# A new written order for the linear-attention and long-convolution kernel, with some VectorE steps moved and the inverse transform's last matmuls split off

## The chip, the cores and the metric

The kernel runs on one core of a Trainium2 chip. The metric is the device time of one execution in microseconds (us), the median of three runs. Before the change it is 296.54 us (runs of 294.0, 296.54 and 297.77). The profile is of one more execution of the same program; its own device time is not listed, its span from the first to the last instruction is 291.2 us.

## The reference, cut to what matters

```python
q, k, v: (8, 8, 576, 64)   w_phi: (64, 128)
w_proj: (512, 1536)        filter_fft: (576, 512)      w_out: (512, 512)

def phi(x):
    proj = x @ w_phi
    proj = proj - max(abs(proj), axis=-1)
    return concatenate([exp(proj), exp(-proj)], axis=-1)
q_p, k_p = phi(q), phi(k)
kv  = einsum('bhsf,bhsd->bhfd', k_p, v);  z = sum(k_p, axis=2)
x   = einsum('bhsf,bhfd->bhsd', q_p, kv) / (einsum('bhsf,bhf->bhs', q_p, z) + 1e-6)
x   = heads side by side, (8, 576, 512)
x1, x2, x3 = split(x @ w_proj, 3)
x2_conv = irfft(rfft(x2, n=576) * rfft(filter_fft, n=576), n=576)     # along the sequence
out = (x1 * x2_conv * x3) @ w_out                                      # float32
```

There are eight batches b. The kernel keeps bf16 operands and float32 sums.

## The kernel before, in words

The 576 positions are split as 64 groups of nine (t, j), and a batch's eight heads lie as four pairs v of heads. The real Fourier transform is a matmul with cosines and sines made on the chip in the opening (the steps `ang`, `frac` and `sin`, lines 420 to 475), folded twice so that only sums and differences of a quarter of the length are multiplied.

The program is one straight list of steps, the string `PLAN`, that `run` (line 1043) goes through once. A word such as `X1e,ACT,2,0@0` calls the method `X1e` with the engine ACT, batch 2 and part 0, on PSUM bank 0. Every step issues its instructions on its engine's queue in this order; each engine runs its own queue in order, and waits on the others by semaphores put in for every tile. So the written order fixes the order on each of TensorE (PE), VectorE (DVE), ScalarE (ACT), GpSimd (POOL) and SyncE (SP), and which PSUM banks are reused after which step. PSUM has eight banks; most steps take two of them in a pair. Most SBUF tiles have rings of two to six buffers (`RING`, line 25), others one.

One batch goes through these steps, those of two or three batches interleaved:

- `load` (GpSimd's queue) brings q, k and v and casts them; `trh` (SyncE's queue, line 607) transposes half of q or k by DMA. In the first batch `pt` and `pte` do that by TensorE and a copy.
- `Pk` (line 636), `Qn` (643), `Pkt` and `Qnt` (651), eight or four matmuls with 64 rows, project k and q. `maxk`, `maxq`, `maxkt`, `maxqt` (VectorE, 716) take the maxima of the absolute values, `ex,k` (ScalarE, 698) both exponentials.
- `mhi`, `mlo`, `trm` and `trme` split q's maxima into two bf16 parts and transpose them; `Pq` and `Pqt` (670 to 687) project q the other way round and subtract the maxima; `ex,q` and `exqt` follow.
- `em` (752) makes k's factors, `vs` (GpSimd, 758) scales v with them, `KV` (773, 72 matmuls of 64 rows) sums over positions, `KVe` copies.
- `NE` and `NEt` (787, 796) make numerator and denominator; `rc` and `xn` (VectorE, 801 and 806), and `rct` and `xnt` for the leftover positions, divide.
- `trx` and `trxt` (SyncE, 825 and 830) transpose the result by DMA for the projections `X1` and `X3` (917) and `X1t` and `X3t` (926).
- `f1` and `f2` (854 and 860) form sums and differences, on GpSimd mostly, and `Ft` (four matmuls of 64 rows, 869) and `Fs` (876) transform; `Fe` and `Xl` copy; `X2` (895) projects in the frequency domain, `Y1` (VectorE, 905) multiplies with the filter, `m3` (909) adds halves.
- `I` (970) transforms back, six matmuls for each quarter m of the features: for each half e two with the main frequencies (T0 and T2) and one with the leftovers T4. T4 holds the leftovers of both halves in its two sets of 64 rows, and `inv[:, 4 + e]` is zero in the rows of the other half. `Ie`, `Ip` and `Im` (988, 991) take sum and difference of the halves.
- `X1e` copies X1, `tm` (958) multiplies with X3, `ym` (1005) with the convolution, `O` (1016) is the last projection, `Oe` copies, `st` stores.

`wz` steps are matmuls on zeros in the opening that keep TensorE occupied. The filter's own transform (`fl_load`, `fa`, `fb`, `rev`, `Ff`, `H`, `He`) runs in the opening too. `fa` (GpSimd, 495) writes its sums `fs` into the memory of `turn`, which holds the angles until the `sin` steps have read them. The index tables `fr` and `nr` have tiles of their own.

Of the kernel before, what the change touches and what calls it, by code (L numbers as in the profile page):

```python
# [36 lines left out]
fl_load,1,1 pt,k,0,1,1@7 exz ex,k,m,0,1@2 maxk,0,0@4 maxq,0,1@0 fl_load,3,1 fl_load,2,0 ex,k,p,0,0@4
pt,k,0,1,0@0 load,v,0 ex,k,m,0,0@4 pt,q,0,1,1@1 load,k,1 fl_load,3,0 maxk,0,1@2 pte,ACT,k,0,1,1@7
fl_load,1,0 pte,DVE,q,0,1,0@6 pte,ACT,k,0,1,0@0 Qn,0,0@4 pte,ACT,q,0,1,1@1 load,q,1 fa,POOL,0
maxq,0,0@4 Pkt,0@6 Qn,0,3@0 trh,k,1,0 maxkt,0@6 ex,k,p,0,1@2 wz,24@4 wz,17@2 trh,q,1,0 Qnt,0@4  # L40
maxq,0,3@0 fa,POOL,1 em,p,0,0 exkt,p,0@6 Pk,0,2@0 exkt,m,0@6 Qn,0,2@2 ex,k,p,0,2@0 maxqt,0@4
Pk,0,3@6 maxq,0,2@2 em,m,0,0 ex,k,m,0,3@6 w_load,proj,2 mhi,0 ex,k,p,0,3@6 rev@4 maxk,0,2@0
vs,POOL,p,0,0 mlo,POOL,0 vs,POOL,m,0,0 ex,k,m,0,2@0 trm,0@2 trme,DVE,0@2 Pq,0,0@2 ex,q,p,0,0@2
Pq,0,1@0 maxk,0,3@6 fb,0@4 em,m,0,1 em,p,0,1 vs,POOL,p,0,1 fb,1@4 wz,11@6 wz,9@7 KV,0,0@6
ex,q,p,0,1@0 ex,q,m,0,1@0 ex,q,m,0,0@2 Pq,0,3@4 Pq,0,2@0 ex,q,m,0,3@4 KVe,DVE,0,0@6 vs,POOL,m,0,1
NE,0,0@6 rc,0,0@6 NE,0,1@2 xn,0,0@6 trh,q,1,1 ex,q,p,0,3@4 Ff,2@6 Pk,1,1@4 rc,0,1@2 xn,0,1@2
f1,POOL,0,0,0 maxk,1,1@4 ex,q,p,0,2@0 Ffe,ACT,2@6 KV,0,1@2 Qn,1,0@6 ex,q,m,0,2@0 wz,5@0
KVe,ACT,0,1@2 ex,k,m,1,1@4 Pk,1,0@2 maxq,1,0@6 ex,k,p,1,1@4 maxk,1,0@2 NE,0,3@0 rc,0,3@0 Ff,3@6
Ffe,ACT,3@6 NE,0,2@4 xn,0,3@0 trh,k,1,1 w_load,proj,0 ex,k,m,1,0@2 Ff,1@6 rc,0,2@4 ptx,0,3@0
xn,0,2@4 ex,k,p,1,0@2 ptx,0,0@1 ptxe,DVE,0,0@1 ptx,0,2@4 f1,POOL,0,0,1 ptxe,DVE,0,3@0 Qnt,1@2  # L50
ptxe,ACT,0,2@4 Ffe,ACT,1@6 maxqt,1@2 Pqt,0@0 exqt,p,0@0 exqt,m,0@0 Qn,1,3@4 Ff,0@6 Ffe,ACT,0@6
Qn,1,2@2 maxq,1,3@4 Pk,1,2@0 Qn,1,1@4 load,v,1 maxq,1,2@2 ex,k,m,1,2@0 maxq,1,1@4 trx,0,1 X1,0,3@6
load,k,2 Pkt,1@2 ex,k,p,1,2@0 w_load,proj,1 maxk,1,2@0 exkt,m,1@2 X1,0,2@7 maxkt,1@2 X1,0,1@4
X1e,ACT,0,2@7 X1e,ACT,0,3@6 mhi,1 NEt,0@0 H,0@5 rct,0@0 xnt,0,1@0 X3,0,1@6 H,3@7 X1e,ACT,0,1@4
f1,POOL,0,1,1 f1,POOL,0,1,0 em,p,1,0 xnt,0,0@0 f2,POOL,0,1,0 tm,0,1@6 load,q,2 f2,POOL,0,1,1
exkt,p,1@2 Ft,0,1,0@2 He,DVE,3,0@7 Fs,0,2@2 Hl,ACT He,DVE,3,1@7 Fs,0,3@0 X1,0,0@4 Fe,ACT,0,2@2
Fe,ACT,0,3@0 Ft,0,0,6@2 He,DVE,0,0@5 X1e,ACT,0,0@4 He,DVE,0,1@5 Pk,1,3@0 f2,POOL,0,0,0 f2,POOL,0,0,1
Fs,0,1@6 Fe,DVE,0,1@6 Fs,0,0@2 H,1@4 ex,k,m,1,3@0 Fe,ACT,0,0@2 He,ACT,1,1@4 X3,0,2@5 He,ACT,1,0@4
mlo,POOL,1 trm,1@6 maxk,1,3@0 em,m,1,0 Xl,DVE,0 trme,DVE,1@6 em,p,1,1 X3,0,0@7 H,2@2 X2,0,2@3
em,m,1,1 ex,k,p,1,3@0 tm,0,0@7 H,4@4 trh,k,2,0 He,DVE,4,0@4 tm,0,2@5 vs,POOL,p,1,0 Pq,1,0@6  # L60
He,ACT,2,0@2 X3,0,3@0 tm,0,3@0 ex,q,m,1,0@6 vs,POOL,m,1,0 KV,1,0@4 vs,POOL,p,1,1 trxt,0
vs,POOL,m,1,1 trh,k,2,1 ex,q,p,1,0@6 Pk,2,0@0 KVe,ACT,1,0@4 Pk,2,1@6 ex,k,p,2,1@6 ex,k,m,2,1@6
trh,q,2,0 late X2,0,3@2 Y1,0,2@3 trh,q,2,1 maxk,2,0@0 X1t,0@3 Y1,0,3@2 maxk,2,1@6 load,v,2 Pq,1,2@4
X1te,ACT,0@3 X2,0,0@3 Y1,0,0@3 X3t,0@2 tmt,0@2 X2,0,1@6 load,q,3 X2,0,4@7 Y1,0,1@6 ex,q,p,1,2@4
Pq,1,1@2 ex,k,p,2,0@0 ex,k,m,2,0@0 Y1,0,4@7 w_load,out ex,q,m,1,2@4 Qn,2,1@0 maxq,2,1@0 ex,q,p,1,1@2
ex,q,m,1,1@2 KV,1,1@4 load,k,3 Qnt,2@6 Pkt,2@0 Pqt,1@2 maxqt,2@6 maxkt,2@0 m3,POOL,0,1 KVe,ACT,1,1@4
exqt,p,1@2 Qn,2,0@6 NE,1,1@4 exqt,m,1@2 maxq,2,0@6 m3,POOL,0,0 rc,1,1@4 xn,1,1@4 I,0,2@2 em,p,2,0
NE,1,0@6 Ie,0,2@2 Im,0,2@2 rc,1,0@6 Ip,0,2@2 exkt,m,2@0 exkt,p,2@0 xn,1,0@6 I,0,0@4 Qn,2,2@2
Ie,0,0@4 Ip,0,0@4 I,0,3@0 vs,POOL,p,2,0 Pq,1,3@6 trh,q,3,1 Ie,0,3@0 ex,q,p,1,3@6 Im,0,0@4
ex,q,m,1,3@6 ym,POOL,0,2 Qn,2,3@4 maxq,2,2@2 Im,0,3@0 I,0,1@2 Ip,0,3@0 maxq,2,3@4 ym,POOL,0,0  # L70
f1,POOL,1,0,0 Ie,0,1@2 Im,0,1@2 NE,1,3@0 rc,1,3@0 Pk,2,3@4 Ip,0,1@2 ym,POOL,0,3 xn,1,3@0 NEt,1@6
trx,1,0 mhi,2 mlo,POOL,2 ex,k,m,2,3@4 NE,1,2@2 em,m,2,0 trm,2@0 trx,1,1 trme,ACT,2@0 Pq,2,1@0
rct,1@6 trh,q,3,0 ex,k,p,2,3@4 ym,POOL,0,1 vs,POOL,m,2,0 xnt,1,0@6 rc,1,2@2 xnt,1,1@6 xn,1,2@2
O,0,1@6 O,0,3@7 trx,1,3 maxk,2,3@4 Pk,2,2@4 ex,q,m,2,1@0 ex,q,p,2,1@0 Oe,DVE,0,1@6 ex,k,p,2,2@4
Qn,3,3@2 Pq,2,2@0 ex,k,m,2,2@4 f1,POOL,1,0,1 maxq,3,3@2 O,0,2@6 Oe,ACT,0,2@6 Oe,ACT,0,3@7
f1,POOL,1,1,1 maxk,2,2@4 load,q,4 KV,2,0@2 KVe,DVE,2,0@2 O,0,0@6 Qn,3,2@4 trx,1,2 Oe,DVE,0,0@6
maxq,3,2@4 Pq,2,0@2 f1,POOL,1,1,0 ex,q,p,2,2@0 X1,1,2@7 ex,q,m,2,2@0 ex,q,m,2,0@2 f2,POOL,1,0,1
trh,k,3,1 X1,1,3@6 ex,q,p,2,0@2 X1e,ACT,1,2@7 st,SP,0,2,1 em,m,2,1 Ft,1,0,4@0 f2,DVE,1,0,0
# [12 lines left out]
tm,1,1@3 rct,2@4 xnt,2,1@4 I,1,2@0 Qnt,3@2 xnt,2,0@4 Pk,3,2@6 ym,POOL,1,1 maxqt,3@2 Ie,1,2@0
Im,1,2@0 Ip,1,2@0 ym,POOL,1,0 X1,2,0@0 ym,POOL,1,2 Pk,3,3@2 Qn,3,1@4 ex,k,m,3,2@6 X1e,ACT,2,0@0
ex,k,p,3,2@6 X1,2,2@1 maxq,3,1@4 X1,2,1@0 mhi,3 f1,POOL,2,1,1 load,v,4 O,1,2@4 maxk,3,3@2
X1e,ACT,2,1@0 Oe,ACT,1,2@4 em,m,3,0 X1e,DVE,2,2@1 trh,k,4,0 maxk,3,2@6 f2,POOL,2,0,0 ex,k,p,3,3@2
O,1,3@0 O,1,0@1 mlo,POOL,3 f2,POOL,2,1,1 f2,POOL,2,1,0 Ft,2,0,6@4 Fs,2,1@6 Oe,ACT,1,0@1 Oe,DVE,1,3@0
Fe,DVE,2,1@6 ex,k,m,3,3@2 X3,2,0@0 tm,2,0@0 trm,3@1 Fs,2,0@4 O,1,1@2 Oe,DVE,1,1@2 vs,POOL,p,3,0
st,SP,1,2,1 vs,POOL,m,3,0 Fe,ACT,2,0@4 trme,ACT,3@1 Qnt,4@4 trh,k,4,1 Ft,2,1,0@6 Fs,2,3@0
Fe,ACT,2,3@0 Fs,2,2@6 em,m,3,1 Pq,3,1@2 vs,POOL,m,3,1 ex,q,m,3,1@2 maxqt,4@4 load,q,5 Qn,4,0@4
Fe,DVE,2,2@6 Pq,3,0@0 ex,q,p,3,0@0 X2,2,3@6 em,p,3,1 ex,q,p,3,1@2 trxt,2 ex,q,m,3,0@0 maxq,4,0@4
Y1,2,3@6 X3,2,1@7 tm,2,1@7 X2,2,2@4 Y1,2,2@4 Xl,ACT,2 trh,k,5,1 KV,3,0@2 Qn,4,2@0 KVe,ACT,3,0@2  # L100
maxq,4,2@0 Pq,3,2@4 Pk,4,1@6 ex,q,m,3,2@4 maxk,4,1@6 X2,2,0@2 ex,q,p,3,2@4 NE,3,1@0 rc,3,1@0
X2,2,1@3 ex,k,p,4,1@6 vs,POOL,p,3,1 xn,3,1@0 ex,k,m,4,1@6 KV,3,1@4 KVe,ACT,3,1@4 Pq,3,3@0 Y1,2,1@3
# [994 lines left out]
```

## Time and profile before

| | us |
|---|---|
| median of three runs | 296.54 |
| lowest, highest run | 294.0, 297.77 |
| the profiled execution's own time | not listed |
| its span | 291.2 |
| busy in it: PE, DVE, ACT, POOL | 274.0, 252.3, 221.9, 228.5 |

A row of the profile's groups gives line, engine, operation, tiles as out<-in, shapes and count, then busy us and mean ns of one, then the engine's idle time before them and what ended it. In the chain that ended last a piece has its start, its length and what ran. In a row of stages each engine has its busy us and the number of its instructions. Matmuls are pipelined, so their durations overlap; the distance between starts is what a step costs TensorE.

### The profile page before, as it was taken

The numbers are of one execution on the slowest core, as the hardware profiler recorded it, in microseconds if no ns is written. First come the engines' busy times: TensorE is split into PE (matmuls) and PEld (weight loads), VectorE is DVE, ScalarE is ACT, GpSimd is POOL, SyncE is SP. The second block draws the span as 40 slices with busy tenths as digits, with TensorE's granted clock in tenths as the row PEclk, the third lists the DMA queues.
The fourth block names the chain that finished last, engine by engine and source line by source line (L and its number), as shares of the span: only waits on it lengthen the run. The fifth ranks groups of instructions, "written<-read, shape, count | busy, mean of one in ns | idle before, by whom it ended". The sixth has DMA issues, their size and how long they took to land.

```text
span 291.2 us, 10275 instructions
## 1 busy us (share of the span) xinstructions
PE 274.0 (94%) x4336; PEld 194.8 (67%) x4336; DVE 252.3 (87%) x438; ACT 221.9 (76%) x367; POOL 228.5 (78%) x187
## 2 busy tenths in 40 slices
PE   6688999998999999999999999999999899999992
...
PEclk9999999999999999999999999999999999999998
...
GB/s 140 230 207 175 144 204 165 139 175 181 143 192 177 163 204 159 153 119 165 122 111 156 197 169 114 163 135 191 99 14 93 84 36 2 34 108 54 69 130 184
DMA packets 72319, 40.07 MB, mean 138 GB/s; under 512 B 52496, under 2 KB 67216, under 8 KB 72272
## 3 DMA queue, kind: packets, MB, share of 16 engines
...
q10 hardware_dynamic: 320, 0.52, 0.7%
...
HBM read 33.75 MB, written 9.44 MB: 148 GB/s over the span
## 4 chain that ended last, share of the span: by engine, by line
PE 71%; DVE 3%; ACT 2%; issue 1%; DVEq 0%; ACTq 0%
PE ps L917 17%; PE ps L895 11%; PE ps L1016 10%; PE ps L970 8%; PE ps L773 5%; PE ps L787 4%; PE ps L876 3%; PE ps L926 2%; PE ps L670 2%; PE ps L636 2%; PE ps L643 2%; PE ps L676 2%; PE ps L869 2%; DVE mq L716 1%; PE ps L796 1%
## 5 line engine op out<-in xcount | busy, mean ns | idle before, releaser
L917 PE MATMUL ps<-xT,wproj 128*128 128x256 bf16 x512 | 64.0, 273 | 0.2 <-DMA wproj<-in_moe_w_proj_dram 0.2
L917 PEld LDWEIGHTS <-wproj 128*128 128x128 bf16 x512 | 48.1, 98 | 9.0 <-DMA wproj<-in_moe_w_proj_dram 0.4
L1005 POOL TENSOR_TENSOR yT<-cv,x1s 128x576 bf16<-128x576 f32 x31 | 39.4, 1279 | 15.6 <-ACT es L988 7.7
L716 DVE TENSOR_REDUCE mq<-ps 128x8 f32<-128x1024 f32 (+1 forms) x40 | 43.7, 1112 | 3.5 <-PE ps L643 1.5
L716 DVE TENSOR_REDUCE mk<-ps 128x8 f32<-128x1024 f32 (+1 forms) x40 | 44.1, 1112 | 2.9 <-PE ps L636 1.6
L758 POOL TENSOR_TENSOR vm<-vn,vm 128x1152 bf16<-128x1152 bf16 x16 | 34.3, 2152 | 7.4 <-ACT vm L752 7.4
L758 POOL TENSOR_TENSOR vp<-vn,vp 128x1152 bf16<-128x1152 bf16 x16 | 34.4, 2155 | 4.6 <-ACT vp L752 4.5
L698 ACT ACTIVATE Eqp<-ps 128x1024 bf16<-128x1024 f32 x32 | 32.9, 1038 | 6.1 <-PE ps L676 6.0
L854 POOL TENSOR_TENSOR SD<-xn 128x512 bf16<-128x512 bf16 x28 | 31.9, 1153 | 6.2 <-DVE xn L806 4.7
L1016 PE MATMUL ps<-wout,yT 128*128 128x512 bf16 x140 | 34.8, 379 | 0.1
L860 POOL TENSOR_TENSOR xf<-SD 128x512 bf16<-128x512 bf16 x26 | 29.7, 1155 | 6.4 <-DVE SD L854 5.9
L698 ACT ACTIVATE Ekp<-ps 128x1024 bf16<-128x1024 f32 x32 | 33.2, 1036 | 1.1 <-PE ps L636 0.7
L698 ACT ACTIVATE Eqm<-ps 128x1024 bf16<-128x1024 f32 x32 | 32.6, 1037 | 1.6 <-PE ps L676 0.8
L698 ACT ACTIVATE Ekm<-ps 128x1024 bf16<-128x1024 f32 x32 | 33.1, 1033 | 0.8 <-PE ps L636 0.7
L895 PE MATMUL ps<-wproj,XF 128*128 128x512 bf16 x128 | 31.6, 379 | 0.3 <-ACT x1s L298 0.3
L991 DVE TENSOR_TENSOR cv<-es,ps 128x288 f32<-128x288 f32 x64 | 26.3, 445 | 5.7 <-ACT es L988 4.4
L909 POOL TENSOR_TENSOR T<-T,T 128x1024 bf16<-128x1024 bf16 x14 | 29.6, 2127 | 1.7 <-DVE r L801 0.8
L970 PE MATMUL ps<-inv,T 128*128 128x288 bf16 x192 | 28.1, 286 | 0.7 <-DVE mq L716 0.4
L958 DVE TENSOR_TENSOR x1s<-ps,x1s 128x512 bf16<-128x512 f32 x32 | 21.8, 685 | 2.5 <-PE ps L917 1.1
L298 ACT COPY o<-ps 128x512 f32<-128x512 f32 x20 | 11.8, 600 | 14.4 <-PE ps L1016 12.0
L806 DVE TENSOR_TENSOR xn<-ps,r 128x512 bf16<-128x512 f32 x32 | 21.9, 689 | 0.9
L298 ACT CAST x1s<-ps 128x512 bf16<-128x512 f32 (+1 forms) x33 | 17.4, 540 | 6.7 <-PE ps L917 3.2
...
## 6 DMA issues: line engine op xcount, KB each, us to landing
...
```

Of the source, the lines that this page charges most:

```text
L298: self.nc.scalar.copy(dst, src)
L698: self.nc.scalar.activation(e, p, AF.Exp, bias=0.0, scale=1.0 if g == "p" else -1.0)
L716: self.nc.vector.tensor_reduce(out=out, in_=src, axis=AX.X, op=ALU.max, apply_absolute_value=True)
L758: self.eng(eng).tensor_tensor(out=t[:, :, :, 0:64], in0=self.at("vn", b)[:, 2 * X:2 * X + 2], in1=t[:, :, :, 64:65].to_broadcast([128, 2, ...
L854: self.eng(eng).tensor_tensor(out=o[:, :, 2 * i:2 * i + 2, :], in0=x[:, :, 0:2, :], in1=x[:, :, 2:4, :], op=ALU.subtract if i else ALU.add)
L860: self.eng(eng).tensor_tensor(out=o[:, :, 2 * i:2 * i + 2, :], in0=x[:, :, 0:4:2, :], in1=x[:, :, 1:4:2, :], op=ALU.subtract if i else ALU ...
L895: self.mm(self.pb(0), l, w[:, kt, 512:1024], start=(kt == 0), stop=(kt == 3))
L909: self.eng(eng).tensor_tensor(out=Y, in0=Y, in1=self.at(f"T{2 * e + 1}", b), op=ALU.add)
L917: self.mm(o[:, d], w[:, kt, f0 + 128 * m:f0 + 128 * m + 128], y[:, 1, ::-1, ::-1] if d else y[:, 0], start=(kt == 0), stop=(kt == 3))
L970: self.mm(self.pb(e, 0, 288), l, inv[:, 2 * e + i if i < 2 else 4 + e, :], start=(i == 0), stop=(i == 2))
L1005: self.eng(eng).tensor_tensor(out=self.at("yT", b)[:, m, 0:SEQ], in0=self.turn_of("cv", (b, m)).rearrange("p x h t -> p (x h t)"), in1=sel ...
L1016: self.mm(self.pb(0), y[:, kt, 128 * c:128 * c + 128], w[:, kt, :], start=(kt == 0), stop=(kt == 3))
```

## The change

The written order is new from the first word to the last; the steps are the same but for these:

- Each of the 32 `I` steps becomes `Is` (the four main matmuls) and, at another place of the order, before or behind it, `It` (16 times) or `Iz` (16 times). `It` takes the leftovers as two matmuls of 64 rows, in different halves of the array; `Iz` as two of 128 rows, as `I` did. `opens` remembers which of the parts came first, and only that one clears the bank. `Ft` and `Fs` may come in either order in the same way.
- Steps on another engine, counted before and after: `Fe` on DVE 7 to 13, on ACT 25 to 19; `X1e` on DVE 7 to 4; `Oe` on DVE 15 to 13; `KVe` on DVE 4 to 3; `pte` on DVE 4 to 6; `trme` on DVE 3 to 5; `Ffe` on DVE 0 to 1; `He` on DVE 5 to 4; `Xl` on DVE 1 to 0; `X1te` on DVE 0 to 1; `yt` on DVE 1 to 2; `f2` on DVE 6 to 2, on POOL 26 to 30; `m3` on DVE 2 to 3, on POOL 14 to 13; `ym` on DVE 1 to 4, on POOL 31 to 28. `f1` stays at 4 on DVE, at other places.
- `fsx` is a tile of its own. `fs` lies in it, and so do `fr` and `nr`.
- In the order, `exz` (the exponential on a dummy) now comes ahead of `sin,9` (the sine on a dummy); k is loaded ahead of q; `trx` stands behind its `xn`, most within a few steps, and loads and transposes stand further ahead of their uses; the stores are spread otherwise.

```diff
 PLAN = """
-gz,DVE sin,9 fz,DVE cz,DVE,0 loadh,q,0,0 gi_nr cz,DVE,1 gi_part gi_col cols_a cols_b cols_h
-loadh,k,0,0 gi_fr ang,DVE,2 wz,23@0 wz,30@1 wz,31@0 wz,32@1 wz,33@0 ang,ACT,3 fl_loadt ident frac,3
...
-Pq,2,3@0 ex,q,p,2,3@0 rc,2,0@4 xn,2,0@4 vs,POOL,m,2,1 Qn,3,0@6 ex,q,m,2,3@0 X2,1,2@2 f1,POOL,2,0,0
...
-trx,2,3 Pkt,3@4 Y1,1,4@2 maxkt,3@4 f2,POOL,2,0,1 X3,1,3@3 maxk,3,0@0 exqt,p,2@6 exkt,p,3@4
-exkt,m,3@4 X1t,1@2 X1te,ACT,1@2 f1,POOL,2,1,0 I,1,3@6 tm,1,3@3 X3t,1@4 I,1,1@2 Ie,1,3@6 em,p,3,0
...
+fl_loadt zeros fz,DVE cz,DVE,1 fl_load,3,0 gi_part gi_col fl_load,1,0 gi_nr loadh,k,0,0 fl_load,0,1
+cz,DVE,0 gz,DVE loadh,q,0,0 exz wz,23@1 cols_a w_load,phi loadh,k,0,1 fl_load,2,1 wz,34@7 fl_load,2,0
...
+xn,2,3@1 Xl,ACT,1 X1,1,1@5 m3,POOL,1,0 maxk,3,1@6 trx,2,3 X1e,ACT,1,0@4 X1e,ACT,1,1@5 NE,2,2@1 X2,1,4@0
...
+f1,POOL,2,1,0 exqt,m,2@6 Pk,3,0@0 exkt,p,3@4 trh,q,4,0 tm,1,3@2 It,1,3@6 exkt,m,3@4 f1,POOL,2,1,1
+Is,1,3@6 maxk,3,0@0 Iz,1,1@2 Ie,1,3@6 Is,1,1@2 trh,q,4,1 Ie,1,1@2 X3t,1@5 f2,POOL,2,0,0 Ip,1,3@6
...
 """
     def gi_fr(self):
-        g, s = self.nc.gpsimd, self.scr
-        self.fr = s.tile([128, 2, 2, 144], FP32, name="fr")
+        g = self.nc.gpsimd
+        self.fr = self.fsx[:, 0:576].rearrange("p (a b x) -> p a b x", a=2, b=2)
...
+    def opens(self, *key):
+        new = key not in self.opened
+        self.opened.add(key)
+        return new
+
     def Ft(self, b, X, bank2):
         xt, Dt = self.at("xnt", b), self.at("Dt")
+        new = [self.opens("F", b, 2 * X + w) for w in range(2)]
         for e in range(2):
             for w in range(2):
                 r, bank = slice(64 * w, 64 * w + 64), bank2 if w else self.bank
                 self.mm(self.ps[:, bank + e, 0:288], xt[r, X, :],
-                        Dt[r, 288 * e:288 * e + 288], start=True, stop=False)
+                        Dt[r, 288 * e:288 * e + 288], start=new[w], stop=not new[w])
...
-    def I(self, b, m):
-        c, inv = slice(128 * m, 128 * m + 128), self.at("inv")
-        for e in range(2):
-            Y = self.at(f"T{2 * e}", b)
-            for i in range(3):
-                l = Y[:, i, c] if i < 2 else self.at("T4", b)[:, c]
-                self.mm(self.pb(e, 0, 288), l, inv[:, 2 * e + i if i < 2 else 4 + e, :],
-                        start=(i == 0), stop=(i == 2))
-
     def It(self, b, m):
-        c, inv = slice(128 * m, 128 * m + 128), self.at("inv")
+        c, inv, new = slice(128 * m, 128 * m + 128), self.at("inv"), self.opens("I", b, m)
         for e in range(2):
             r = slice(64 * e, 64 * e + 64)
-            self.mm(self.pb(e, 0, 288), self.at("T4", b)[r, c], inv[r, 4 + e, :], start=True,
-                    stop=False)
+            self.mm(self.pb(e, 0, 288), self.at("T4", b)[r, c], inv[r, 4 + e, :], start=new,
+                    stop=not new)
+
+    def Iz(self, b, m):
+        c, inv, new = slice(128 * m, 128 * m + 128), self.at("inv"), self.opens("I", b, m)
+        for e in range(2):
+            self.mm(self.pb(e, 0, 288), self.at("T4", b)[:, c], inv[:, 4 + e, :], start=new,
+                    stop=not new)
 
     def Is(self, b, m):
-        c, inv = slice(128 * m, 128 * m + 128), self.at("inv")
+        c, inv, new = slice(128 * m, 128 * m + 128), self.at("inv"), self.opens("I", b, m)
         for e in range(2):
             for i in range(2):
                 self.mm(self.pb(e, 0, 288), self.at(f"T{2 * e}", b)[:, i, c],
-                        inv[:, 2 * e + i, :], start=False, stop=(i == 1))
+                        inv[:, 2 * e + i, :], start=new and i == 0, stop=not new and i == 1)
...
-        self.fs = self.turn.rearrange("p a x -> p (a x)")[:, 0:2048].rearrange(
-            "p (a x) -> p a x", a=4)
+        self.fsx = s.tile([128, 2048], FP32, name="fsx")
+        self.fs = self.fsx.rearrange("p (a x) -> p a x", a=4)
```

More of the change, by code (lines that the diff above doesn't have):

```diff
@@ L37 @@
[L37 to L78, printed above, removed]
@@ L91 @@
[L91 to L102, printed above, removed]
@@ new lines @@
+cz,DVE,0 gz,DVE loadh,q,0,0 exz wz,23@1 cols_a w_load,phi loadh,k,0,1 fl_load,2,1 wz,34@7 fl_load,2,0
+wz,11@0 cols_b ang,DVE,2 fl_load,1,1 gi_fr ang,ACT,3 gi_back loadh,q,0,1 ang,DVE,0 fl_load,3,1 wz,30@5
+frac,2 wz,32@3 fl_load,0,0 load,v,0 back frac,0 wz,5@4 frac,3 wz,33@3 sin,9 sin,2 wz,18@6 sin,0
+ang,DVE,1 frac,1 ident sin,1 w_phi pt,k,0,0,0@6 one wz,0@5 cols_h pte,DVE,k,0,0,0@6 wz,24@0 pt,k,0,0,1@3
+sin,3 Pk,0,0@4 pte,DVE,k,0,0,1@3 wz,17@0 maxk,0,0@4 wz,35@0 pt,q,0,0,0@1 fa,POOL,1 pt,q,0,0,1@2
```

273 lines of the change are left out of this document (160 added, 113 removed).

## The prediction

> **What bounds the kernel now.** I read the page first, then the busy time of every engine by stage, then the chain that ended last, then single rows.
>
> ```profile
> span 291.2 us, 10275 instructions
> PE 274.0 (94%) x4336; PEld 194.8 (67%) x4336; DVE 252.3 (87%) x438; ACT 221.9 (76%) x367; POOL 228.5 (78%) x187
> PE   6688999998999999999999999999999899999992
> PEclk9999999999999999999999999999999999999998
> ```
>
> The span is full of TensorE work except at its two ends, and the granted clock never drops before the last slice. Only shorter TensorE work or fewer TensorE holes can change the time. The stages say where the holes are (columns: stretch and its length, busy time of PE, PEld, DVE, ACT, POOL, clock, DMA):
>
> ```profile
> 0.00:20.00 20.00, 13.80 (x134) 6.81 (x134) 17.12 (x71) 15.42 (x25) 14.25 (x27) 1.00 1.01 191
> 20.00:40.00 20.00, 17.80 (x378) 12.55 (x375) 17.41 (x24) 20.00 (x30) 16.77 (x15) 1.00 1.26 171
> 40.00:50.00 10.00, 10.00 (x117) 8.22 (x116) 9.63 (x16) 9.42 (x22) 5.90 (x6) 1.00 1.26 182
> 50.00:80.00 30.00, 27.71 (x573) 19.55 (x572) 28.14 (x44) 27.08 (x43) 29.43 (x22) 1.00 1.13 159
> 80.00:220.00 140.00, 139.98 (x2228) 101.58 (x2226) 125.59 (x192) 110.67 (x186) 120.83 (x89) 1.00 0.95 148
> 220.00:232.00 12.00, 11.07 (x255) 8.59 (x253) 11.57 (x22) 10.75 (x17) 10.35 (x9) 1.00 0.31 64
> 232.00:280.00 48.00, 48.00 (x639) 35.00 (x638) 38.89 (x68) 26.92 (x48) 30.94 (x23) 1.00 0.30 59
> 280.00:291.20 11.20, 5.66 (x30) 2.54 (x27) 3.91 (x8) 1.66 (x3) 0.00 (x0) 0.90 0.66 167
> ```
>
> From 80 to 220 us TensorE is idle 0.02 of 140 us: there nothing but TensorE's own work counts. Its holes are 6.2 us before 20, 2.2 to 40, 2.3 from 50 to 80, 0.9 from 220 to 232, and 5.5 in the last stage. In the opening ScalarE runs without a pause (20.00 of 20 us from 20 to 40), and VectorE is busy 17.12 + 17.41 + 9.63 + 28.14 = 72.3 of the first 80 us. So the opening is held by these two engines, the long middle by TensorE, the end by the last stores.
>
> **The inverse leftovers apart (I becomes Is with It or Iz).** The number of matmuls is the same. Sixteen of the 32 leftovers become It: two matmuls on 64 rows each, in different halves of the array, in place of two on 128 rows. The price of a half-array stretch beside full-array ones is in the chain, and the nearest thing to It is the frequency leftover Ft, four matmuls of 64 rows by 288:
>
> ```profile
> 128.65 0.47 PE ps L926 x16
> 129.12 0.46 PE ps L796 x8
> 129.58 0.73 PE ps L970 x6
> 130.32 0.86 PE ps L1016 x4
> 131.18 0.87 PE ps L917 x8
> 132.05 0.33 PE ps L636 x8
> 132.38 0.22 PE ps L643 x8
> 132.61 0.84 PE ps L970 x6
> 133.45 0.66 PE ps L917 x6
> ```
> ```profile
> 193.64 0.42 PE L869 MATMUL ps<-Dt,xnt 64*128 64x288 bf16 x4
> 193.99 0.64 PE L926 MATMUL ps<-xTt,wproj 128*128 128x64 bf16 x16
> ```
>
> An I step (L970) takes 0.73 us, 0.122 a matmul, behind another 128-row step (L796), and 0.84 behind a 64-row one (Qn, L643). Pk (L636), eight matmuls of 64 rows, takes 0.33 behind a 128-row step, and Qn, as large, 0.22 behind Pk. So every change of row mode costs about 0.10 us, in both directions. Ft starts at 193.64 and its follower at 193.99: 0.35 us, which is one change (0.10) and 0.25 for four matmuls, so two of them run side by side at 0.122 a pair. It therefore saves one pass, 16 x 0.12 = 1.9 us. But I counted the changes of row mode in both written orders: 140 before, 156 after, 16 x 0.10 = 1.6 us more. Net **-0.3 us**. Bounds: -1.9 if all new changes fall where TensorE waits anyway, +1.6 if It's halves do not pair; Ft says that they pair. Iz is the old third matmul moved, and the freedom to put Is before or after costs nothing by itself; Ft and Fs only change who opens the bank.
>
> **The swaps of engine.** These rows price them (mean ns is the second number):
>
> ```profile
> L300 DVE COPY o<-ps 128x512 f32<-128x512 f32 x15 | 10.3, 685 | 3.3 <-PE ps L1016 3.2
> L298 ACT COPY o<-ps 128x512 f32<-128x512 f32 x20 | 11.8, 600 | 14.4 <-PE ps L1016 12.0
> L860 DVE TENSOR_TENSOR xf<-SD 128x512 bf16<-128x512 bf16 x6 | 2.3, 416 | 0.0
> L860 POOL TENSOR_TENSOR xf<-SD 128x512 bf16<-128x512 bf16 x26 | 29.7, 1155 | 6.4 <-DVE SD L854 5.9
> L300 DVE CAST XF<-ps 128x576 bf16<-128x576 f32 x7 | 5.2, 753 | 2.6 <-PE ps L876 2.6
> L300 DVE COPY mT<-ps 128x128 bf16<-128x128 bf16 x3 | 0.7, 219 | 0.2 <-PE ps L744 0.2
> L909 DVE TENSOR_TENSOR T<-T,T 128x1024 bf16<-128x1024 bf16 x2 | 1.3, 683 | 0.0
> L1005 DVE TENSOR_TENSOR yT<-cv,x1s 128x576 bf16<-128x576 f32 x1 | 0.8, 759 | 0.0
> L758 POOL TENSOR_TENSOR vp<-vn,vp 128x1152 bf16<-128x1152 bf16 x16 | 34.4, 2155 | 4.6 <-ACT vp L752 4.5
> ```
>
> Up to the step X1,1,2 (TensorE reaches it at about 80 us now), VectorE gets nine copies and evacuations that were ScalarE's (two pte, Ffe, two Fe, one He, trme, two Oe) and gives five back (trme, two He, Xl, KVe): four more at about 0.69, **+2.7 us** of VectorE, and -4 x 0.60 = -2.4 of ScalarE. Its 7.7 us of idle time in the first 80 must cover that. Later the swaps on VectorE come to less than 1 us over all, under full TensorE work, which hides them while VectorE (125.59 of 140 us busy) and GpSimd (120.83) keep their slack; without that cover they would cost that 1 us. The input loads on GpSimd's queue are the same ones in another order, under the same cover. The two-operand steps are 13 on VectorE before (six f2, four f1, two m3, one ym) and 13 after (two f2, four f1, three m3, four ym). They go where GpSimd waits for their result anyway: the m3 of batch 4 and the f1 of batch 5 stand behind GpSimd's last m3 and ahead of its f2. I take 0; if a step met a GpSimd operation and had to wait it out, 2.2 us (the vp row), and then only where VectorE has no slack.
>
> The Trainium skill (GPSIMD Engine Reference, Key points) says that GpSimd shares its SBUF interfaces with VectorE and meets contention from instructions with two SBUF inputs; no such pair overlaps in this trace, so no run here shows it.
>
> **The opening.** Three things change. GpSimd's filter sums (fa) now write to memory of their own, so they need not wait until the sine steps have read the angles; k is loaded ahead of q, behind three short index steps of GpSimd that now come after the first load; and the exponential's dummy step comes ahead of the sine's, so ScalarE must change its table three times, not twice.
>
> ```profile
> 0.74 1.28 ACT L460 ACT_TABLE_LOAD   x1 [0.74 <-PEq L1081]
> 11.34 1.28 ACT L701 ACT_TABLE_LOAD   x1
> 12.63 0.20 ACT L701 ACTIVATE ez<-zz 128x1 bf16<-128x1 bf16 x1
> 12.74 1.01 ACT L698 ACTIVATE Ekm<-ps 128x1024 bf16<-128x1024 f32 x1
> 13.36 4.65 POOL L495 TENSOR_TENSOR turn<-fl 128x1024 f32<-128x1024 f32 x2 [4.53 <-ACT ez L701]
> ```
>
> The first of them falls in ScalarE's idle time; the last still stands in front of the first real exponential, and the middle one in front of the sines. So ScalarE's stream of exponentials, the thing that runs without a pause from 20 to 40, starts up to 1.28 us later, but has 2.4 us less of other work to carry: -1.1 in sum. GpSimd's 4.53 us wait goes; the vs steps behind it wait for VectorE's maxima, not for fa, so only a part of it comes through. VectorE has 2.7 us more. Bounds for the opening: +2.7 (VectorE is the one that counts, and all its waits stay) to -5.0 (the 7.7 us of idle VectorE time less the 2.7 are the most that can be squeezed out). I take **-1.0**, nearer to the ScalarE sum, because ScalarE is the engine without a pause.
>
> By the Trainium skill (ScalarE: Activation LUTs, What ACT_TABLE_LOAD costs) each change of table is followed by a drain of 1.38 us, which would make the extra load 2.66 and the sum 1.4 us worse. The trace differs: the next ScalarE step starts at 12.63, 0.01 us behind the end of the load.
>
> **The transfers.** The order on SyncE's queue puts each transpose of xn right behind the step that makes its input and stores further back. What a transfer's distance is worth:
>
> ```profile
> DMA to landing us min/median/max: 2.4/4.2/6.2
> 74.66 2.55 SPq L825 DMA_TRANSPOSE xT<-xn  x2
> 79.79 1.89 PE ps L917 x16
> ```
>
> The second of the two transposes issued from 74.66 on goes out at about 75.9; with a median 4.2 us it lands at about 80, at the moment at which TensorE uses it. So in this execution late transfers cost nearly nothing, but they have no slack: an execution in which they take two more would stop TensorE. That fits the three times, 294.0, 296.54 and 297.77, which lie further apart than any other uncertain thing here. Adding this trace's TensorE steps between a transpose and its first use in the written order, the smallest distance grows from 0.0 to 4.4 us for xn, and from 2.8 to 6.3 for q and k. SyncE's instructions are in order, so a transpose that waits for xn holds the stores and transposes of k and q behind it; the stores wait for nobody soon, the transposes have the larger distances to lend. I take **0** for the profile and **-0.6** for the median; bounds 0 and -2.5 (median less lowest).
>
> **220 to 232 us.** VectorE is busy 11.57 of 12 us there. The new order takes two output copies and an f2 from it (0.69 + 0.69 + 0.42) and gives it an Fe (0.75) and a trme (0.22): -0.8. TensorE's hole is 0.9. I take **-0.5**. **The end:** the last matmuls, copies and stores are as many; a half-width store fewer stands behind the last copy, **-0.2**, bounds -0.6 and +0.6 (one output copy less or more ahead of the last store).
>
> **The sum** against the profile: 291.2 - 0.3 - 1.0 - 0.5 - 0.2 = 289.2, and -0.6 for transfers in the median. The profiled execution's own time is not given; its span lies 2.8 under the lowest and 5.3 under the median of the runs shown. I carry the differences to the median: 296.54 - 2.0 - 0.6 = **293.9 us**.
>
> **Rivals.** (a) *All of it is hidden* (18%): TensorE bounds the middle, the opening moves its waits about. For it: 0.02 us of holes from 80 to 220. Against: 11.6 us of holes before 232. It leaves -0.3: **296.2**. (b) *The opening really closes up* (17%): half of the 8.4 us of holes before 40, all of the 2.3 and the 0.9, and the 2.5 us between median and lowest: -9.9 + 1.0 that VectorE cannot spare: **287.6**. For it: the written distances grow almost everywhere. Against: VectorE is 90% busy there and is given more. (c) *VectorE becomes the bound of the opening* (15%), the one on the other side: its 2.7 us come on top, since its idle time lies in waits for loads, TensorE and the start. Price +2.7 - 0.3, and up to 1.28 more for the table: 299 to **300.2**. It decides once VectorE's idle time in the first 80 us cannot fall below its present 7.7. (d) That the change does not do what it says is small: the overlap of It rests on Ft, and without it the sum is 1.9 worse, within my range.
>
> **Numbers.** The forecast has 50%. Two per cent, about what a measurement of this kernel can tell from no change, is 5.9 us. Faster than 290.6 is (b) and an edge of the forecast, 0.19; slower than 302.5 would be (c) with lost transfers besides, 0.05; the rest is 0.76. The range runs from the upper part of (b) to (c): 288.5 to 299.5.
>
> **What would show it.** In the changed profile: It's two matmuls start together and cost about 0.12; fa starts before 13 us; three table loads; TensorE full from 80 to 220 us again with the same busy time; holes from 50 to 80 under 2.3 us and VectorE still over 28 of 30 there. I am wrong if the holes of the opening shrink by more than 4 us, or if the middle shows waits on transposes or on VectorE.

## The result, and the profile after

The changed kernel took 308.65 us (median of 4 runs, 305.28 to 314.06), the kernel before 295.27 beside it: ratio 1.0455, 95% interval 1.0359 to 1.0550. Forecast were 293.9 us and no measurable change. Every ratio leaves out executions more than 1.5% above the fastest of their kernel, which the medians given with it include; the profiled execution, 314.06 us, is one of these, so what is read from it is the upper end of the loss. A second measurement of the same kernel (run e12 below: 302.06 us, ratio 1.0249, interval 1.0177 to 1.0321) shows what of it is steady. All eight executions lie between 301.42 and 314.06.

The page of the profile after, the rows that answer to those of before:

```profile
span 312.3 us, 10247 instructions
PE 275.5 (88%) x4302; PEld 196.7 (63%) x4336; DVE 257.9 (83%) x443; ACT 224.8 (72%) x363; POOL 226.7 (73%) x187
PE   6668633899989998997999899999999999999993
PEclk9999775699999999999999999999999999999998
```

TensorE is busy about as long (275.5 us against 274.0; 34 matmul records are missing here), but the row of slices has a pit, 6 3 3, at 31 to 55 us, and the granted clock falls to 7 7 5 6 from 31 to 62 us. Before, both rows ran through. The stages (stretch and length; busy time of PE, PEld, DVE, ACT, POOL; clock; DMA):

```profile
20.00:40.00 20.00, 15.17 (x323) 10.96 (x318) 15.44 (x21) 17.16 (x26) 17.66 (x14) 0.91 1.26 179
40.00:50.00 10.00, 2.31 (x48) 1.73 (x48) 3.05 (x5) 2.84 (x5) 2.26 (x2) 0.68 1.35 144
50.00:80.00 30.00, 26.26 (x412) 19.31 (x412) 22.68 (x29) 22.74 (x39) 17.98 (x14) 0.82 0.86 123
80.00:220.00 140.00, 133.07 (x2216) 97.69 (x2229) 124.36 (x197) 111.30 (x180) 121.67 (x94) 1.00 0.92 144
```

From 40 to 50 us every engine stands (2 to 3 us busy of 10 each); only the transfers work (1.35). So no engine became the bound: all wait for transfers. What TensorE waited for from 10 to 70 us (total, times, longest):

```profile
PE ps L632 <- DMA kT<-kn: 8.7, 2, 6.9
PE ps L920 <- DMA xT<-xn: 3.2, 1, 3.2
```

The transposes of k and of xn are late. Why they are late stands on GpSimd's queue. Before, it issued the loads of the second batch's k and q ahead of the filter sums fa (L495, quoted in the prediction):

```profile
7.34 0.75 POOL L596 DMA_DIRECT2D kn<-in_k_dram  x1
8.07 0.76 POOL L596 DMA_DIRECT2D qn<-in_q_dram  x1
```

After, behind them (fa is L491 here):

```profile
6.08 0.77 POOL L592 DMA_DIRECT2D vn<-in_v_dram  x1
14.97 2.35 POOL L491 TENSOR_TENSOR fsx<-fl 128x1024 f32<-128x1024 f32 x1 [8.12 <-DMA fl<-in_moe_filter_fft_dram]
17.27 0.77 POOL L592 DMA_DIRECT2D kn<-in_k_dram  x1
18.03 0.76 POOL L592 DMA_DIRECT2D qn<-in_q_dram  x1
```

Note the 8.12: fa has memory of its own now, but it still needs the filter, whose last piece comes at 14.7 us. GpSimd issues its instructions in order here, so the two loads behind fa wait with it, although they need nothing of the filter. They go out 10 us later; k's transposes follow later, and one that went out at 28.2 us and landed in 6.1 (first row, before) goes out at 35.7, straight ahead of three input loads of 576 KB, and lands in 13.9 (second row, after):

```profile
DMA to landing us min/median/max: 6.1/6.1/6.1
```
```profile
DMA to landing us min/median/max: 13.9/13.9/13.9
```

The hole has a second price. The same columns as above, in short stretches:

```profile
42.00:44.00 2.00, 0.40 (x4) 0.23 (x4) 1.32 (x2) 1.19 (x3) 1.73 (x2) 0.91 1.28 130
44.00:46.00 2.00, 0.00 (x0) 0.00 (x0) 0.00 (x0) 0.00 (x0) 0.53 (x1) 0.50 1.24 180
50.00:52.00 2.00, 2.00 (x26) 1.28 (x22) 1.22 (x1) 1.29 (x2) 0.00 (x0) 0.50 1.22 200
58.00:60.00 2.00, 2.00 (x14) 1.34 (x14) 0.00 (x0) 1.06 (x4) 1.75 (x3) 0.50 0.00 0
60.00:62.00 2.00, 2.00 (x24) 1.72 (x25) 1.91 (x4) 1.75 (x4) 1.83 (x2) 0.82 0.00 0
```

The hole begins at 42.6 us. About 1.0 us into it, at 43.6, the clock goes to half, and it stays there until about 60.7, 11 us after work came back at 49.6, with one more hole in between. TensorE counts as full from 56 to 60 us, but eight matmuls of X1 take 1.91 us there (from 57.65), and 1.03 behind it (from 61.14).

To divide the loss: TensorE's row at X1,1,2 and its last row, before, after, and in run e5 below.

```profile
79.72 1.52 PE L917 MATMUL ps<-xT,wproj 128*128 128x256 bf16 x12
284.73 1.04 PE L1025 MATMUL ps<-wout,yT 128*128 128x256 bf16 x8
```
```profile
97.92 1.27 PE L920 MATMUL ps<-xT,wproj 128*128 128x256 bf16 x10
306.32 0.60 PE L1025 MATMUL ps<-wout,yT 128*128 128x256 bf16 x4
```
```profile
80.70 1.49 PE L920 MATMUL ps<-xT,wproj 128*128 128x256 bf16 x12
288.65 0.60 PE L1025 MATMUL ps<-wout,yT 128*128 128x256 bf16 x4
```

Up to X1,1,2: 79.7 before, 97.9 after, 18.2 us lost. From there to the last matmul's end: 285.8 - 79.7 = 206.1 before, 306.9 - 97.9 = 209.0 after, 2.9 lost. The stores behind it take as long as before. In the second measurement the shares are 3.6 and 5.9 us (X1,1,2 at 83.3 us): the pit was missed, but the middle was worse.

### The profile page after: what moved, and what is told of

Same layout as the page of the kernel before. It is cut to its first block, busy times and chain, and to the rows that moved or that the text cites. A ratio compares the mean times of both kernels' runs of the same rounds, so it can differ in the third digit from the quotient of the medians.

```text
span 312.3 us, 10247 instructions
## 1 busy us (share of the span) xinstructions
PE 275.5 (88%) x4302; PEld 196.7 (63%) x4336; DVE 257.9 (83%) x443; ACT 224.8 (72%) x363; POOL 226.7 (73%) x187
## 4 chain that ended last, share of the span: by engine, by line
PE 55%; DVE 5%; DMA 4%; issue 3%; POOL 3%; ACT 2%; SPq 0%; DVEq 0%; ACTq 0%
PE ps L920 13%; PE ps L1016 8%; PE ps L898 8%; PE ps L769 4%; PE ps L984 4%; PE ps L783 3%; DMA xT<-xn 3%; PE ps L879 2%; PE ps L929 2%; PE ps L666 2%; PE ps L871 1%; PE ps L672 1%; PE ps L632 1%; PE ps L639 1%; DVE T L908 1%
## 5 line engine op out<-in xcount | busy, mean ns | idle before, releaser
L920 PE MATMUL ps<-xT,wproj 128*128 128x256 bf16 x512 | 65.2, 277 | 4.5 <-DMA xT<-xn 4.4
L920 PEld LDWEIGHTS <-wproj 128*128 128x128 bf16 x512 | 49.0, 99 | 13.8 <-issue 5.2
L856 POOL TENSOR_TENSOR xf<-SD 128x512 bf16<-128x512 bf16 x30 | 34.1, 1151 | 13.2 <-DVE r L797 7.4
L1005 POOL TENSOR_TENSOR yT<-cv,x1s 128x576 bf16<-128x576 f32 x28 | 35.5, 1276 | 7.4 <-DVE cv L991 4.8
L1016 PE MATMUL ps<-wout,yT 128*128 128x512 bf16 x125 | 33.3, 380 | 0.9
L294 ACT CAST x1s<-ps 128x512 bf16<-128x512 f32 (+1 forms) x35 | 19.0, 548 | 18.0 <-PE ps L920 15.6
L898 PE MATMUL ps<-wproj,XF 128*128 128x512 bf16 x116 | 30.4, 380 | 1.1 <-ACT x1s L294 0.4
L912 POOL TENSOR_TENSOR T<-T,T 128x1024 bf16<-128x1024 bf16 x13 | 27.3, 2122 | 1.5 <-DVE T L908 1.5
L783 PE MATMUL ps<-KVs,Eqp 128*128 128x65 bf16 x256 | 19.8, 193 | 1.7 <-ACT Eqp L694 1.1
L908 DVE TENSOR_TENSOR T<-ps,HTo 128x1024 bf16<-128x1024 f32 x16 | 19.2, 1218 | 2.0 <-PE ps L898 1.9
```

What stands on the lines that cost most here:

```text
L783: self.mm(self.pb(u, 65 * a, 65 * a + 65), E, KVs[:, u, v, s, :], start=(s == 0), stop=(s == 1))
L856: self.eng(eng).tensor_tensor(out=o[:, :, 2 * i:2 * i + 2, :], in0=x[:, :, 0:4:2, :], in1=x[:, :, 1:4:2, :], op=ALU.subtract if i else ALU ...
L898: self.mm(self.pb(0), l, w[:, kt, 512:1024], start=(kt == 0), stop=(kt == 3))
L912: self.eng(eng).tensor_tensor(out=Y, in0=Y, in1=self.at(f"T{2 * e + 1}", b), op=ALU.add)
L920: self.mm(o[:, d], w[:, kt, f0 + 128 * m:f0 + 128 * m + 128], y[:, 1, ::-1, ::-1] if d else y[:, 0], start=(kt == 0), stop=(kt == 3))
L1005: self.eng(eng).tensor_tensor(out=self.at("yT", b)[:, m, 0:SEQ], in0=self.turn_of("cv", (b, m)).rearrange("p x h t -> p (x h t)"), in1=sel ...
```

## The experiments

A ratio is to the kernel before, run beside it; the intervals are 95%. Kernels made from the changed one have its line numbers (Pk L632, KV L769, X1 and X3 L920), those made from the kernel before its own (L636, L773, L917).

### The loads behind fa

**e1**, the changed kernel with the two loads ahead of fa again:

```diff
-load,v,0 ... fa,POOL,1 ... load,k,1 ... load,q,1
+load,v,0 load,k,1 load,q,1 ... fa,POOL,1
```

> The changed kernel with load,k,1 and load,q,1 moved on POOL from behind fa,POOL,1 to right behind load,v,0. Theory A (fa waits 8.12 us for the filter and holds the issue of the two loads back, 17.27 and 18.03 us in place of 7.34 and 8.07 us; the transposes of the second batch are late, PE stands 1.7, 7.0 and 3.2 us and runs at half the granted clock behind it): the holes of 1.7 and 7.0 us go, X1 of the first batch starts near 40 us in place of 52, and the time is 291 to 296 us. Theory B (the transposes are late because the three loads of the third batch start beside them, at 36.05 to 37.55 us): the transposes still meet these loads, the hole of 7 us stays, and the time is 301 or more. Theory C (the steps of the engines in the new opening cost it): 303 to 308, as before.

300.06 us, ratio 1.0193 (1.0126 to 1.0260). The pit is gone, X1 of the first batch starts at 44.6 us in place of 52.2; but 300 is above theory A's 296. Against the first measurement of the changed kernel (1.0455) the gain is clear; against the second (1.0249, from 1.0177) the intervals overlap, so by itself this run does not show it.

**e2**, the other way round, in the kernel before:

```diff
-load,k,1 ... load,q,1 fa,POOL,0 ... fa,POOL,1
+fa,POOL,0 fa,POOL,1 load,k,1 load,q,1
```

> The kernel before, with fa,POOL,1 and behind it load,k,1 and load,q,1 moved to right behind fa,POOL,0, so that POOL issues the two loads behind both halves of fa, near 18.0 and 18.8 us in place of 7.34 and 8.07 us, as in the changed kernel. Theory A: the loads land near 25 and 28 us in place of 21.4 and 23.9, the transposes run into the loads behind them, and the time rises by 6 to 14 us, to 301 to 309. Theories B and C: 294 to 298.

307.35 us, ratio 1.0421 (1.0338 to 1.0503): as much as the whole loss of the first measurement, out of the old order, by two loads behind fa. TensorE's waits from 25 to 70 us are those of the changed kernel:

```profile
PE ps L636 <- DMA kT<-kn: 5.8, 2, 3.9
PE ps L917 <- DMA xT<-xn: 3.2, 1, 3.2
```

**e4**, the changed kernel with the next three loads kept away from the late transposes:

```diff
-load,k,2 ... load,v,1 ... load,q,2 ... f1,POOL,0,1,1
+f1,POOL,0,1,1 load,k,2 load,v,1 load,q,2
```

> The changed kernel with load,k,2, load,v,1 and load,q,2 moved on POOL behind f1,POOL,0,1,1; everything else stays, so load,k,1 and load,q,1 are as late as there. Theory B: trh,k,1,1 and trx,0,1 land in 6 to 8 us in place of 13.9 and 18.4 us, the holes of 7.0 and 3.2 us go, and the time is 292 to 297 us. Theory A: trh,k,1,1 is still issued at 35.7 us in place of 28.2, so PE waits 1 to 3 us in place of 7 and the time is 297 to 302 us. Theory C: 303 to 308 us.

307.06 us, ratio 1.0361 (1.0296 to 1.0425). The time is outside theories A and B and inside the range of theory C, but not for its reason, for what TensorE waits for is a transfer again. The transposes of theory B landed as it said (7.6 and 6.5 us) and the holes of the first batch did go (X1 at 42.1 us), but the loads put off are missed one batch later; from 55 to 80 us:

```profile
PE ps L639 <- DMA qT<-qn: 6.9, 1, 6.9
```

That transpose of q took 14.2 us to land, beside the loads of v, w_out, q and k issued from 54.8 to 59.2 us. Moving loads behind one transpose puts them in front of the next. So late and crowded are one chain here, and e1 and e2 put its beginning at fa.

**e3** was to price the clock alone, with warming matmuls on zeros in the places where TensorE waits:

```diff
+wz,40@4 (x4) ahead of Pk,1,1; wz,41@0 (x17) ahead of Pk,1,2; wz,42@2 (x9) ahead of X1,0,3
```

> The changed kernel with warming matmuls (wz) put in where PE waits: 4 ahead of Pk,1,1, 17 ahead of Pk,1,2 and 9 ahead of X1,0,3. The transposes come no earlier; only the granted clock behind the holes is kept up. If the half clock is a price of its own, the granted clock stays 1.0 from 30 to 65 us and the work that ran at 0.50 to 0.84 (about 14 us busy) is some 6 to 7 us shorter: 300 to 302 us. If the time is set by the transposes and by the other engines alone: 306 to 309 us.

315.89 us, ratio 1.0605 (1.0539 to 1.0670). In its profile the late transposes were others (6.8 us at Qnt, before the warming steps), so these came behind the hole and cost their own time, 34 matmuls in 9.23 us. It doesn't price the clock, and no run here does. That the place of the hole changes, e12 shows for one and the same kernel.

**e12**, the changed kernel again.

> The changed kernel itself once more, beside the others on this chip: 304 to 310 us, ratio 1.036 to 1.055 to the kernel before. Its profile should again show PE standing for a transpose of k or q and for the transpose of xn between 31 and 58 us, with a granted clock of 0.5 behind them; place and length may differ, since they hang on how the transfers meet.

302.06 us, lower than expected. In the profiled execution fa started at 14.4 us and the loads went out 0.6 us sooner than in the first profile. The k transpose was issued at 30.4 in place of 35.7 us and landed at 39.9, not 49.5, ahead of the three input loads behind it, and there was neither pit nor half clock from 20 to 80 us. So the loss differs widely between executions of one program, by how the transfers meet; that the 0.6 us decided it is likely, not shown.

### What the first repair left: a cast beside GpSimd

In e1 TensorE waited 2.3 us for a copy of q that VectorE made late. VectorE's timeline, then GpSimd's:

```profile
16.41 3.25 DVE L296 CAST f<-flt 64x512 bf16<-64x512 f32 x1
```
```profile
17.02 2.35 POOL L491 TENSOR_TENSOR fsx<-fl 128x1024 f32<-128x1024 f32 x1
```

The cast ends 0.3 us after fa. It does so in each of the five profiles in which it stands beside an fa (the changed kernel twice, e1, e3, e4): 0.28 to 0.29 us behind that fa's end, whether it took 0.46 or 3.25 us. In the kernel before, where GpSimd did nothing beside it, it took 0.40 (first row), and again 0.41 in **e5** (second row), which moved it to a stretch in which GpSimd waits:

```profile
10.52 0.40 DVE L300 CAST f<-flt 64x512 bf16<-64x512 f32 x1
```
```profile
9.32 0.41 DVE L296 CAST f<-flt 64x512 bf16<-64x512 f32 x1
```
```diff
 (e1, and)
-fa,POOL,1 ... ft,DVE
+ident ft,DVE ... fa,POOL,1
```

> The run with the loads first, and ft,DVE (the cast of f) moved from behind fa,POOL,1 to behind ident, where GpSimd has nothing to do. Theory P (the cast reads and writes SBUF and is held by a GpSimd operation that runs beside it: 3.26 us in the run with the loads first, 0.40 in the kernel before, where none ran): the cast takes 0.4 us, the evacuation of q behind it comes 2.9 us earlier, PE's hole of 2.3 us before Qn,0,3 and the granted clock of 0.82 behind it go, and the time falls by 2 to 4 us against the run with the loads first, to 1.005 to 1.012 of the kernel before. Rival (VectorE's own work sets the opening, the cast lies beside it): within 1 us of the run with the loads first, ratio 1.017 to 1.021.

295.70 us, ratio 1.0064 (1.0043 to 1.0085), as theory P had it. Three moved steps out of the whole new order, the two loads and the cast, bring 4.55% (2.49% in the second measurement) down to 0.64%. By the Trainium skill (VectorE: DVE Perf Modes, Mode 2x_2P) a copy with one source, from SBUF to SBUF, can use both of VectorE's read ports; GpSimd shares its SBUF interfaces with VectorE and contends with such two-port instructions (GPSIMD Engine Reference, Key points). The trace agrees: 3.25 against 0.40.

### Single parts of the change, on e5

**e6**, no half rows:

```diff
-It,b,m   (all 16)
+Iz,b,m
```

> The run with the cast early, with every It made Iz: all 32 inverse leftovers go over 128 rows, two matmuls one after the other, none over 64 rows side by side. If It saves a pass of 0.12 us each time and costs nothing: slower by 1 to 2 us than the run with the cast early. If, as the prediction has it, the changes of row mode eat most of it: within 0.5 us either way. If a change of row mode costs more than the pass: faster by up to 1 us.

297.29 us, ratio 1.0122 (1.0086 to 1.0158): 1.6 us above e5's median, and the intervals just fail to meet. But e7 below, which lacks no more than a dummy step, lies as far above e5, so the medians don't settle it. In e5, It and Iz, 16 steps each:

```profile
L977 PE MATMUL ps<-inv,T 128*128 128x288 bf16 x32 | 6.4, 286 | 0.0
L971 PE MATMUL ps<-inv,T 64*128 64x288 bf16 x32 | 3.7, 286 | 0.2 <-ACT Fqm L706 0.2
```

It's pairs do run together: 2.7 us less busy time. What the row changes take back can be read from the profiles. From X1,1,2 to the last matmul TensorE is busy 202.2 us and idle 6.4 in e5, busy 203.6 and idle 4.3 in e6, with as many matmul records. So the half rows leave about 1.4 us less work, row changes included, and that execution of e5 lost it to waits.

**e7**, without the dummy exponential exz.

> The run with the cast early, without the dummy exponential exz, so that ScalarE loads two tables, not three. If the third load is on the path of the sines: 0.5 to 1.3 us faster than the run with the cast early. If the sines wait for VectorE's angles anyway: within 0.4 us of it.

297.27 us, ratio 1.0124 (1.0085 to 1.0162). The expectation doesn't apply: there were still three table loads, as the angles' own step now asked for the first.

**e8**, the kernel before with fs in memory of its own (fr and nr share it), its order unchanged.

> The kernel before, whose order stays, with fs and the index rows in memory of their own as in the changed kernel, so that fa waits for the filter alone, which lands at 13.05 us, and not for the sines. The prediction's term for the opening: fa starts at about 13.1 in place of 13.36 us and little follows: ratio 0.996 to 1.003. If the wait for the sines held the opening: 1 us or more faster, 0.990 to 0.996.

294.58 us, ratio 1.0020 (0.9990 to 1.0050). fa started at 13.28 in place of 13.36 us, now waiting 4.47 us for the filter in place of 4.53 for the sines. The wait for the sines had cost nothing that these runs resolve.

**e9**, e5 with all 69 changed engine assignments put back.

> The run with the cast early, in its order, with every step that the change gave to another engine (69 copies, evacuations and two-operand steps between VectorE, ScalarE and GpSimd) put back on the engine it had before. If the swaps cost the opening what the prediction worked out for VectorE (2.7 us) and ScalarE does not pay for it: 1 to 2.7 us faster than the run with the cast early, ratio to the kernel before 0.997 to 1.003. If they are neutral, as the forecast took them: within 0.7 us. If the order was made for the new engines: slower by 1 us or more.

303.64 us, ratio 1.0319 (1.0274 to 1.0363): about 8 us worse than e5, although VectorE is busy 68.9 us of the first 80 in place of 73.9. The new order needs the new engines; which of the 69 matter was not separated, and the swaps' price on VectorE alone says nothing.

### Where the last per cent is: the middle

TensorE's waits from 75 to 300 us, before (all of them), then in the second measurement of the changed kernel (the two largest):

```profile
PE ps L787 <- ACT Eqm L698: 0.3, 1, 0.3
```
```profile
PE ps L920 <- DMA xT<-xn: 2.2, 1, 2.2
PE ps L769 <- issue: 1.9, 2, 1.0
```

Two new waits: one on a transpose of xn, and one in KV for which the profile has no releaser ("issue").

**e10**, e5 with one load moved from just ahead of that transpose, and **e11**, e10 with ident moved ahead of VectorE's angle steps:

```diff
-load,v,3 ... ym,POOL,1,1          e11: -frac,1 ident
+ym,POOL,1,1 load,v,3                   +cols_b ident
```

> The run with the cast early, with load,v,3 moved on POOL behind ym,POOL,1,1, some 7 us later, so that the transpose trx,2,2 has no load started just ahead of it. It took 8.6 us to land there and held X1,2,0 for 1.5 us. If the neighbour's load makes the transpose slow: it lands in 3 to 6 us, the hole at X1,2,0 goes, 0.5 to 1.5 us faster than the run with the cast early. If the two transposes of q behind it, on the same queue, do: landing and hole stay, within 0.5 us.

> The run with v later, and ident moved on VectorE from behind frac,1 to behind cols_b (9.2 us to about 4 us). PE waits 1.6 us for ident before the first transposes of k, while VectorE, which must copy them out, is at work without a pause until 10.3 us. If VectorE's own work sets the opening: PE's wait for ident goes and a wait for the copies takes its place, within 0.4 us of the run with v later. If the transposes set it: 1 to 1.5 us faster.

297.58 (1.0095; 1.0054 to 1.0136) and 296.86 (1.0063; 1.0021 to 1.0104). The transpose trx,2,2 landed in 2.6 us in place of 8.6 and X1,2,0 no longer waits, yet the time did not fall; an unnamed wait of 1.6 us came up later. In e11 the wait for ident went (1.6 us in e5's profile, 0.3 in e10's) and 0.7 us for VectorE's copies came in its place; the medians of e10 and e11 can't be told apart.

The unnamed waits have a pattern. Counted through TensorE's weight loads, those in the profiles of e1 to e12 behind 80 us stand at numbers 991, 1759, 1887, 2015, 2399 and 2527: all 95 + 128 n. And the page of the profile has a queue that fits, in the changed kernel as before:

```profile
q8 instruction: 34, 0.56, 0.8%
```

34 packets of 0.56 MB / 34 = 16.5 KB for 2 x 4336 loads and matmuls: an estimate of 255 instructions a packet. So the waits seem to stand where TensorE passes from one block of its instructions to the next, and each ends some 1.2 to 1.6 us behind the end of a packet of this queue. If that packet starts late, and the block before it is a dense one (KV has 72 matmuls in 1.1 us), TensorE would run out of instructions. **e14** tries this in the kernel before, where there is no such wait, by one load:

```diff
-load,k,7 ... m3,POOL,3,0 load,q,6
+load,k,7 load,q,6 ... m3,POOL,3,0
```

> The kernel before, with load,q,6 moved on POOL from behind m3,POOL,3,0 (issued at 154.3 us) to right behind load,k,7 (about 145.4 us), so that it is in flight when TensorE crosses the border of an instruction block near 149.4 us and needs the next block 4.4 us later. Nothing uses it sooner. Theory R: the packet of the instruction queue starts 3 to 4 us behind the border in place of 0.7, TensorE has an unnamed wait of 0.5 to 1.5 us near 154 us, where the kernel before has none. Rival: no such wait, ratio 0.998 to 1.002.

296.83 us, ratio 1.0121 (1.0068 to 1.0174). The load goes out at 145.26 in place of 154.25, and TensorE stops in the midst of KV:

```profile
155.20 0.19 PE L773 MATMUL ps<-vp,Fkp 64*128 64x65 bf16 x1 [1.35 <-issue]
```

The queues from 150.0 to 151.2 us before (packets, MB, share), then in e14 from 149.2 to 152.4 and from 152.4 to 153.8:

```profile
q1 hardware_dynamic: 315, 0.18, 71.5%
q8 instruction: 1, 0.02, 7.1%
```
```profile
q0 software_dynamic: 586, 0.66, 120.6%
q14 instruction: 1, 0.01, 0.6%
```
```profile
q1 hardware_dynamic: 601, 0.25, 205.7%
q0 software_dynamic: 37, 0.03, 11.9%
q8 instruction: 1, 0.02, 5.7%
```

Before, the packet came 0.7 us behind the block's border (150.1 against 149.4 us); with the input load in flight it came 3.2 us behind it (152.45 against 149.26), when the load was through, and TensorE stood until 1.5 us after its end. The span of this profile is 1.7 us longer than that of before, and 1.35 of it is this wait; what the rest of the 1.2% consists of is not shown. **e13** is the reverse, e10 with three loads taken out of such stretches:

```diff
-load,v,4 (117.2 us)    load,q,7 (153.7)   load,q,6 (156.6)
+load,q,5 load,v,4 ... m3,POOL,3,1 load,q,6 load,q,7
```

> The run with v later, and besides load,v,4 right behind load,q,5, and load,q,6 and load,q,7 behind m3,POOL,3,1, so that fewer input loads are in flight while TensorE works through KV and its neighbours of batches 3 and 4. Theory R (TensorE's unnamed waits are refills of its instructions, a packet of the instruction queue that starts late because input loads are in flight): the refill in the KV of batch 4 starts within 1.5 us of its block's border, in place of 3.4 to 3.8, the unnamed wait there goes, and those of batch 3 shrink: 0.5 to 2 us faster than the run with v later. If the loads have nothing to do with them: the same waits, within 0.5 us.

296.80 us, ratio 1.0047 (1.0006 to 1.0089), 0.8 us below e10, with overlapping intervals. The waits of e10 at weight loads 1887 and 2015 went, and one of 2.8 us appeared a block earlier, at 122 us. (The wait in the KV of batch 4, at 2399, stands in e5's profile and no longer in e10's.) A load that is moved away from one border comes to lie on another. No version tried here beats the kernel before.

## Why the prediction was wrong, point by point

- **The bound** was read rightly: the opening is where the order decides, and the middle has no slack in TensorE. It followed that any new wait in the middle counts in full; that was not put into the sum, and the middle lost 2.9 us in the first profile and 5.9 in the second.
- **The input loads** is the step that failed. It said that they "are the same ones in another order, under the same cover". Two of them had moved behind an instruction that waits for another transfer until 14.97 us, and nothing covered that; the term stood at nothing without a row for it. e2 measures the step by itself: +4.2%.
- **The opening**, -1.0: "GpSimd's 4.53 us wait goes" was wrong. fa waited 8.12 us, since memory of its own frees it from the sines, not from the filter; e8 shows +0.2% (-0.1 to +0.5) for that part alone. In place of -1.0 the opening lost 18.2 us in the first profile and 3.6 in the second. With the loads and the cast put right it is still not shorter: 80.7 us against 79.7. The third table load did no harm: the first real exponential starts at 12.67 us against 12.74.
- **Two-operand steps**: the 0 holds for them (yT 755 ns on VectorE against 759; none ran beside a GpSimd operation). The bound of 2.2 us was right in kind but hung on the wrong instruction: a cast with one operand was held by fa, 2.85 us in e1 and 0.7 in the first profile (1.13 against 0.40).
- **The transfers**, 0 and -0.6: wrong in sign. The distance from a transpose to its use grew in the written order, as worked out, but the landing time is no constant: 2.3 to 18.4 us within the first profile, the longest ones beside input loads. X1,2,0 waited on xn's transpose in six of the profiles of the new order, and not in that of before.
- **The leftovers**, -0.3: TensorE's work fell by about 1.4 us by the profiles of e5 and e6, so the row changes took back less than the 1.6 us worked out; the medians don't resolve it. **The swaps**, 0, can't be had one by one (e9).
- **220 to 232 us**, -0.5, and **the end**, -0.2: neither came. The work of that stretch lies about 20 us later in the first profile, and the hole went along: TensorE is idle 0.87 of the 13 us from 241 on, where it was idle 0.93 of 12, and VectorE is as full there as before (12.58 of 13 us). The stores behind the last matmul take as long as before.
- **The rivals**: the slower one, VectorE as the bound, is not what happened: from 40 to 50 us VectorE stands too. A rival in which a transfer's issue is held up on GpSimd's queue was missing; the list of signs ("the middle shows waits on transposes") would have caught it. Of the other signs, the three table loads came; fa before 13 us, the full middle and a busy VectorE from 50 to 80 us (22.68 of 30) did not.
